# A transfer in four parts, and GpSimd work fenced against VectorE's operations, in a kernel of long convolution and linear attention

## The chip, the cores and the metric

The kernel runs on one core of one Trainium2 chip. TensorE (PE, with its weight loads as PEld), VectorE (DVE), ScalarE (ACT), GpSimd (POOL) and SyncE (SP) run their own queues of instructions in order and wait for each other by semaphores; SP issues every transfer of this kernel. The metric is the device time of one launch in microseconds. Three runs of the kernel before gave 248.29, 248.36 and 249.4; the median is 248.36.

## The reference

Two independent halves work on sequences of S = 2048 positions and D = 576 channels, and are set side by side in the output. All inputs are bfloat16.

```
A:  k_shift = sum over t<4 of k delayed by t, times shift_k[:, t]
    kv = k_shift * v
    y  = causal convolution of kv with ssm_k along S (by FFT of length 2S) + kv * ssm_D
    out[:, :576] = q * y
B:  q, k, v = x @ wqkv, 32 heads of 18
    phi(t) = (t+1 if t>0 else exp(t)) + 1e-6
    num = phi(q) (phi(k)^T v),  den = phi(q) . sum(phi(k)) + 1e-6
    out[:, 576:] = (num / den) @ wo
```

## The kernel before

**Half A.** Channels are cut into five pieces (`HP`): four of 128 and one of 64. For each piece and each half of the positions, `conv_piece` makes four tap products at once (L413, "tap"), adds them in two steps (L418 "tap+", L421, called "tapx" here), and multiplies by v (L424, "tapv"). The convolution is a transform in two stages. `s1` multiplies by the table Gsb on PE (L501) and copies out of PSUM ("s1ev"); `s2` transposes blocks on DVE (L518) and does a small transform on PE (L527). For the filter the same happens ("h": L451, then s1), with a transposing transfer ("trq", L476) and L484 in place of the block transpose for the pieces of `HDMA`. The spectra are then worked on in nine slices of 64 channels, g = 0 to 8: `inv` has two transfers exchange the filter spectrum's rows within SBUF ("X"), makes two products of 128 x 2048 (L548, "p0" and "p1", on DVE or POOL), and transforms back on PE (L558, "i1"), copied into U[vg] ("i1ev").

Slices 0 to 3 fill U0, slices 4 to 7 fill U1, each 128 x 8192 elements (2 MB). In U the partition is 32 kh + something, and the next stage needs another index on the partitions. So `inv2` turns the corner by way of DRAM: one transfer writes U[vg] to `v_scr` (L595, "Vw"), four read it back in another order into V[vg] (L599, "Vr"). Then i2 on PE with table Esb (L611) and the product with q on DVE (L621, "i2q"), and two stores ("yo"). Slice 8 has its own short way without DRAM.

**Half B.** `kproj` and `qproj` (L644, L662) are matmuls of five; phi is an Exp on ACT (L647, L670) and one DVE operation with min and max (L650 "kphi", L673 "qphi"). `b_G` makes G = x^T phi(k) in ten groups of sixteen matmuls (L700, evacuated at L712 or L714). From it come kv, z, den and its reciprocal (L799), M, and broadcasts of the reciprocal ("bc", L827). EPS is added to phi(q): for four of nine tiles by POOL ("pqe", L845), which then multiplies by the copied broadcast ("pqg", L837), for the others within one DVE operation (L841). `b_out` makes sixteen row blocks of the output, two groups of five matmuls each (L861, "out"), copied to `ob` on ACT or DVE ("oev") and stored ("oo").

**What sets the order.** Every piece of work is an entry of a program with a number. The strings PLAN, PLACES and FILL at the end of the file give the order of all entries with the engine of each (P, A, D, G for POOL, S for SP), the place of every buffer, and how many filler matmuls on a zero tile `fz` (L909) stand ahead of an entry. They were made by a planner from the costs written beside each entry, such as `_dve(n)` or `TPOOL`; nothing of it is decided at run time. So an engine that waits holds up all that is behind it in its queue. Two entries by line:

```
595:  load("Vw", None, lambda e: dma(ap(V_d[vg], 0, [[32 * n, 4], [128 * n, 32], [1, 32 * n]]),
596:                                 U[vg].t[:].rearrange("p k c -> p (k c)")), 8192 * n, rd=[U[vg]],
845:  P.op(("POOL", TPE), lambda e, c=c, gp=gp: nc.gpsimd.tensor_scalar_add(out=pq(c, gp), in0=pq(c, gp), scalar1=EPS),
```

Of the kernel before, what the change touches and what calls it, by code (L numbers as in the profile page):

```python
# [15 lines left out]
EPS = 1e-6  # L16
# [189 lines left out]
def _dve(n, rate=1):  # L206
    return 0.145 + n * 0.001045 / rate


def _dma(nb, row=4096):  # L210
    return nb / (16.0 * row / (8.0 + row * 0.0412) * 1000.0)
# [3 lines left out]
def kernel(  # L215
# [45 lines left out]

    def psb(banks, name):
        return P.buf(name, [128, banks, 512], FP32, space="ps", banks=banks)
# [3 lines left out]
    neg1 = SB("neg1", [128, 1], FP32, side=1, pre=True)  # L267
    Gsb = SB("Gsb", [128, 16, 2, 128], side=1, pre=True)
# [133 lines left out]
    def conv_piece(pc, bh):  # L402
# [4 lines left out]
        def tap(e):  # L407
            base = kb.t[:, 8 * bh:8 * bh + 8, c0:c0 + n]
            i0 = bass.AP(tensor=base.tensor, offset=base.offset,
                         ap=[list(base.ap[0]), [D, 4], [D, 8], [1, n]])  # L410
            w = Wj.t[:, 3:4, c0:c0 + n]
            i1 = bass.AP(tensor=w.tensor, offset=w.offset, ap=[list(w.ap[0]), [-D, 4], [0, 8], [1, n]])
            nc.vector.tensor_tensor(out=m.t[:], in0=i0, in1=i1, op=ALU.mult)  # L413
# [3 lines left out]
        P.op(("DVE", _dve(16 * n, 2)),  # L417
             lambda e: nc.vector.tensor_tensor(out=m.t[:, 0:2], in0=m.t[:, 0:2], in1=m.t[:, 2:4], op=ALU.add),  # L418
             wr=[m], name="tap+", bias=bias)
        P.op(("DVE", _dve(8 * n, 2)),  # L420
             lambda e: nc.vector.tensor_tensor(out=m.t[:, 0], in0=m.t[:, 0], in1=m.t[:, 1], op=ALU.add),  # L421
             wr=[m], name="tap+", bias=bias)
        P.op(("DVE", _dve(8 * n, 2)),
             lambda e: nc.vector.tensor_tensor(out=vt.t[:, 8 * bh:8 * bh + 8, c0:c0 + n], in0=m.t[:, 0],  # L424
# [116 lines left out]
    def inv(g, su, bias):  # L541
# [5 lines left out]
        for x, wr in ((1, [(tx, ("x", 0)), (tx, ("x", 1))]), (0, [(tx, 0), (tx, 1)])):  # L547
            P.op({"DVE": _dve(2048, 2), "POOL": TPOOL}, lambda e, x=x: (nc.vector if e == "DVE" else nc.gpsimd).tensor_tensor(  # L548
# [38 lines left out]
    def inv2(vg, bias):  # L587
# [5 lines left out]
        if vg in DR:  # L593
            dtok = P.buf("vd%d" % vg, [128, 1], space="dram")
            load("Vw", None, lambda e: dma(ap(V_d[vg], 0, [[32 * n, 4], [128 * n, 32], [1, 32 * n]]),  # L595
                                           U[vg].t[:].rearrange("p k c -> p (k c)")), 8192 * n, rd=[U[vg]],
                 wr=[dtok], bias=bias, row=8192)
# [246 lines left out]
    for c, gp in PQG:  # L844
        P.op(("POOL", TPE), lambda e, c=c, gp=gp: nc.gpsimd.tensor_scalar_add(out=pq(c, gp), in0=pq(c, gp), scalar1=EPS),  # L845
             wr=[(pqT, (c, 2 * gp + i)) for i in range(2)], name="pqe", bias=("bc", 0.0))
# [42 lines left out]
    P.op(("POOL", 0.35), lambda e: nc.gpsimd.memset(fz.t[:], 0.0), wr=[fz], name="fz", bias=1200)  # L889
# [7 lines left out]
    with tc.manual_schedule():  # L897
        cnt = 0
        for o in order:
# [10 lines left out]
            o.fn(o.eng)  # L910


T16 = 0.28
TPOOL = 4.9
TPQ = 2.6
TPE = 1.3
# [4 lines left out]
9:10 416:3 105:9 99:2 33:9 150:3 444:1 474:1 471:1 451:1 549:1 294:2 309:1 501:2 518:1 568:1 602:2 336:2 598:1 651:1  # L921
703:1 692:7
# [3 lines left out]
G5 S6 G8 G13 S7 S406 S52 G1 S53 G95 G2 S54 G3 S32 G717 S18 G4 S15 P9 S14 P11 S31 A10 A12 P407 G277 S16 P409 D408 A410  # L926
S17 D411 P416 S19 P412 S45 A417 P414 P418 D415 A413 S44 P25 P23 P26 P22 A419 S42 D27 P28 G0 S20 D24 A29 D420 G30 S47
P105 D424 P111 A106 P114 D107 A112 P96 D113 A115 P102 D116 A97 S428 D55 P117 A103 P421 A118 P108 A423 D104 A422 P99
D56 S43 A109 A100 D98 D57 D110 P33 S534 D58 P34 S46 P36 A35 P39 D101 P526 D59 P37 A40 P522 A38 P120 A527 D119 P129 D60
S478 A121 G41 P425 A130 D122 A427 D61 P150 S429 D75 A426 P141 P132 A151 S545 G48 A142 P135 S546 A133 P156 D143 A523  # L930
D134 D76 P138 A136 A157 S49 P147 D137 A139 D77 P144 A148 D140 P123 A145 D78 D146 P126 D131 A124 G271 D62 S535 P162 S50
A127 D125 D79 P240 A163 S273 P180 A241 P430 D149 A181 D128 P432 A431 D182 P174 D80 A433 P183 S272 P186 D434 A175 D158
P171 A184 D81 A187 P177 D185 A172 D176 P168 S275 A178 G51 D173 D188 P195 A169 D179 D164 P204 S453 A196 D170 D152 P210
A205 D82 P524 A211 D206 P207 A525 D87 P213 A208 P198 A214 P528 D215 A199 D212 P192 A529 D209 D200 P216 D88 A193 P189
S454 A217 P165 D194 A190 D218 S710 D89 P225 A166 S479 D197 P222 A226 D90 P159 A223 D227 S503 D224 P455 D167 A160 P457
D191 A456 P219 D161 P201 D530 A458 A220 P480 D459 D242 A202 P482 D221 A481 P228 D203 S21 D483 P531 A229 D484 D541 P237
A533 D230 P231 S662 A532 D91 P153 A238 G537 S274 P243 A232 D92 A154 D239 P542 D155 A244 P259 D233 A544 D245 D93 A543
D71 P251 D94 G547 D72 D73 P246 D74 D252 A253 D83 P266 D247 D248 D84 G536 P256 D267 A268 D85 D86 P234 D63 A257 A260
A258 P504 A235 P261 A505 D236 G548 D64 P506 A262 A263 P254 D508 D65 A507 D66 D67 P509 A255 P515 P513 P511 A514 P264
A512 D516 S276 D68 P460 A265 P466 A461 D510 P464 D69 P249 A467 D70 S517 A465 P437 D250 P439 D438 P441 A440 P435 D442  # L940
P462 A436 P491 D463 A492 P554 S443 P487 A555 P552 D488 P556 A553 P489 D557 P485 A490 P558 S468 D486 P269 A559 D571
P646 A270 P538 D560 S473 A647 P584 A539 P586 D540 A587 P444 D585 P446 A445 P582 S493 D447 A583 P588 P278 A589 D590
P561 S448 P282 A562 D601 P642 A643 P474 D280 D281 A563 D283 P644 D279 P648 D645 A475 P471 S564 P476 D649 S565 S498
D472 P469 A477 P284 A470 D650 P572 D285 G300 S606 D286 A573 S594 P451 D574 P449 G303 A452 P496 D450 P494 A497 G567
D287 P549 S576 A495 S575 P292 A551 S686 P296 S625 A293 S624 P294 A297 P288 A295 P290 A289 P298 D550 G578 A291 P309
S605 A299 P322 D577 P499 A310 S595 P312 D323 A500 P306 D313 A307 P501 P316 A502 P324 D566 P304 G308 A317 P520 S635
D325 S636 A521 P518 D305 P314 A519 P614 G302 D315 P319 A615 S654 P616 S655 D320 G301 P612 A617 P618 D613 A619 P579
G311 A581 D580 P568 A569 D570 P602 A604 P336 D620 S663 P333 A603 P326 D337 D334 G608 P338 D607 A327 P331 P621 D339
A332 P341 D631 S340 A622 S335 P328 D342 A623 P632 D329 P343 D634 S330 A633 P358 A344 P356 D626 G637 A359 S345 P591
A357 P348 D638 A593 S360 P351 S667 A592 S666 D349 P609 D352 S664 D627 P361 A610 P363 D611 A362 P628 A364 G318 P353  # L950
S365 D596 A630 S665 P346 A629 P681 D597 P683 A347 P639 A354 D684 S350 P679 S355 D682 A640 P677 D680 G321 A641 P598
D678 P668 S685 A599 D600 P670 P651 D671 S687 P386 D669 A652 P672 D653 P674 P371 D673 G656 P403 A372 D657 P383 P381
A384 D404 D387 P391 A382 D675 P401 S385 A392 S676 P398 D402 P376 D399 P396 A377 P660 A397 S400 P658 A661 S689 S691
# [49 lines left out]
```

## Time and profile before

| what | before |
|---|---|
| median of three runs | 248.36 us |
| profiled execution, its own time | 247.67 us |
| its span | 245.8 us |
| PE busy, share of the span | 168.9 us, 69% |
| DVE busy | 175.2 us, 71% |
| ACT busy | 124.2 us, 51% |
| POOL busy | 71.4 us, 29% |
| moved by DMA | 40.51 MB, mean 165 GB/s |
| mean granted TensorE clock | 0.886 |

The busy shares are means over stages with different limits. A line of the chain that ended last reads: start, length, what. In a group's line stand source line, engine, operation, what it writes and reads, shapes and count, then busy time and mean length in ns of one, and the idle time before it. The DMA share is the mean busy share of sixteen DMA engines; it can pass 1 where packets overlap.

### The profile page before, as it was taken

What the parts mean: (1) busy time and instruction counts of PE and PEld (TensorE: products, weight loads), DVE (VectorE), ACT (ScalarE), POOL (GpSimd) and SP (SyncE); (2) the same over time, 40 slices, a digit from 0 to 9 for tenths busy, and PEclk for the clock granted to TensorE, in tenths of its full rate; (3) what the DMA queues carried; (4) which work ended last, traced back from release to release, by engine and by line L of the source; (5) the groups of instructions that cost most, each with busy time, mean ns of one, the idle gap of its engine ahead of it and who ended that gap; (6) DMA issues with size and microseconds to landing.
All of it is one profiled execution on the core that took longest, in us unless ns stands there. A gap on an engine that the chain in (4) does not pass through costs nothing.

```text
span 245.8 us, 4335 instructions
## 1 busy us (share of the span) xinstructions
PE 168.9 (69%) x1777; PEld 113.6 (46%) x1787; DVE 175.2 (71%) x192; ACT 124.2 (51%) x173; POOL 71.4 (29%) x37
## 2 busy tenths in 40 slices
PE   2979798999939169999977866774302968700390
PEld 1666563766517046888733433542101546600270
DVE  0179998999999988979899999799600794000352
ACT  2558796787950004488989999472400621300110
POOL 9010000000099900000019999759200060000000
PEclk9999999999997858999999999997955897965568
DMA  5999998993390000199997932243227834222895
GB/s 162 321 333 362 328 296 208 218 214 90 96 265 0 0 3 0 21 225 150 203 200 232 286 149 98 53 112 109 83 83 229 266 97 120 75 91 101 241 288 186
DMA packets 51144, 40.51 MB, mean 165 GB/s; under 512 B 25204, under 2 KB 47989, under 8 KB 50229
## 3 DMA queue, kind: packets, MB, share of 16 engines
q1 hardware_dynamic: 51124, 40.24, 61.3%
q8 instruction: 14, 0.23, 0.4%
q14 instruction: 6, 0.04, 0.1%
HBM read 21.62 MB, written 8.91 MB: 124 GB/s over the span
## 4 chain that ended last, share of the span: by engine, by line
DMA 39%; PE 23%; DVE 22%; issue 6%; ACT 6%; SPq 1%; DVEq 0%; ACTq 0%
DMA v_scr<-U 26%; PE ps_all L700 7%; DVE m L413 5%; DMA kb<-in_A_k_dram 5%; PE ps_all L501 4%; DMA V<-v_scr 3%; PE ps_all L611 3%; DMA Gsb<-tab_g 3%; DVE pk L650 3%; DVE pqT L673 3%; DVE v L424 3%; DMA xT<-in_B_x_dram 2%; DVE m L418 2%; PE ps_all L644 2%; PE ps_all L662 2%
## 5 line engine op out<-in xcount | busy, mean ns | idle before, releaser
L548 POOL TENSOR_TENSOR TT<-su,TT 128x2048 bf16<-128x2048 bf16 x9 | 40.6, 4524 | 47.7 <-issue 24.3
L611 PE MATMUL ps_all<-V,Esb 128*128 128x256 bf16 x64 | 11.3, 338 | 32.7 <-DMA V<-v_scr 32.7
L700 PE MATMUL ps_all<-pk,x_sb 128*128 128x288 bf16 (+1 forms) x160 | 25.5, 326 | 11.1 <-ACT GT L712 7.2
L861 PE MATMUL ps_all<-M,pqT 128*128 128x288 bf16 x128 | 23.9, 319 | 8.5 <-DVE ob L257 6.8
L255 ACT ACTIVATE ob<-ps_all 128x288 bf16<-128x288 f32 x20 | 7.9, 412 | 40.9 <-PE ps_all L861 21.5
L621 DVE TENSOR_TENSOR q<-ps_all,q 128x512 bf16<-128x512 f32 x18 | 11.7, 685 | 21.8 <-PE ps_all L611 21.8
L700 PEld LDWEIGHTS <-x_sb 128*128 128x128 bf16 x160 | 17.4, 110 | 18.0 <-issue 11.5
L548 DVE TENSOR_TENSOR TT<-su,TT 128x2048 bf16<-128x2048 bf16 x9 | 25.0, 2790 | 0.0
L413 DVE TENSOR_TENSOR m<-kb,Wj 128x4096 bf16<-128x4096 bf16 (+1 forms) x10 | 24.6, 2457 | 0.3 <-DMA kb<-in_A_k_dram 0.2
L611 PEld LDWEIGHTS <-Esb 128*128 128x128 bf16 x64 | 7.3, 118 | 36.5 <-issue 19.1
L845 POOL TENSOR_SCALAR pqT<-pqT 128x1024 bf16<-128x1024 bf16 x4 | 11.1, 2770 | 43.1 <-DVE TT L257 42.8
L644 PE MATMUL ps_all<-wk,xT 128*128 128x288 bf16 x160 | 22.0, 286 | 0.8 <-DMA wk<-in_B_wqkv_dram 0.8
L257 DVE CAST ob<-ps_all 128x288 bf16<-128x288 f32 x12 | 5.1, 446 | 24.4 <-DMA out_dram<-ob 21.4
L861 PEld LDWEIGHTS <-pqT 128*128 128x128 bf16 x128 | 13.2, 107 | 15.3 <-issue 9.1
L501 PEld LDWEIGHTS <-Gsb 128*128 128x128 bf16 x320 | 17.9, 99 | 3.8 <-issue 2.7
L255 ACT ACTIVATE U<-ps_all 128x1024 bf16<-128x1024 f32 x10 | 10.1, 1027 | 17.7 <-PE ps_all L558 17.6
L662 PE MATMUL ps_all<-xT,wq 128*128 128x512 bf16 x74 | 18.6, 379 | 0.4
L255 ACT ACTIVATE TT<-ps_all 128x1024 bf16<-128x1024 f32 x15 | 18.0, 1261 | 0.9 <-PE ps_all L484 0.9
L644 PEld LDWEIGHTS <-xT 128*128 128x128 bf16 x160 | 15.3, 98 | 6.4 <-issue 1.5
L909 PE MATMUL ps_all<-fz 128*128 128x256 bf16 x62 | 11.8, 303 | 8.7 <-POOL fz L889 4.4
L647 ACT ACTIVATE ek<-ps_all,neg 128x288 bf16<-128x288 f32 x32 | 15.4, 507 | 3.3 <-PE ps_all L644 2.5
L255 ACT ACTIVATE su<-ps_all 128x1024 bf16<-128x1024 f32 x15 | 14.8, 1022 | 3.1 <-PE ps_all L527 3.0
(99 smaller groups left out, 324.8 us busy)
## 6 DMA issues: line engine op xcount, KB each, us to landing
TT<-TT SPq DMA_DIRECT2D x18, 256.0 KB, 3.0
v_scr<-U SPq DMA_DIRECT2D x2, 2048.0 KB
V<-v_scr SPq DMA_DIRECT2D x8, 512.0 KB, 5.1
x_sb<-in_B_x_dram SPq DMA_DIRECT2D x4, 576.0 KB, 10.4
kb<-in_A_k_dram SPq DMA_DIRECT2D x2, 1152.0 KB, 11.1
v<-in_A_v_dram SPq DMA_DIRECT2D x2, 1152.0 KB, 11.3
out_dram<-ob SPq DMA_DIRECT2D x16, 144.0 KB, 6.1
q<-in_A_q_dram SPq DMA_DIRECT2D x2, 1024.0 KB, 7.0
```

The lines of the kernel that those rows point to most:

```text
L255: nc.scalar.activation(out=o, in_=i, func=ACTF.Copy)
L413: nc.vector.tensor_tensor(out=m.t[:], in0=i0, in1=i1, op=ALU.mult)
L501: nc.tensor.matmul(pf[:, n * j:n * j + n], lhsT=Gsb.t[:, 8 * bg + j, ri, :], rhs=src(8 * bg + j), start=True, stop=True)
L548: P.op({"DVE": _dve(2048, 2), "POOL": TPOOL}, lambda e, x=x: (nc.vector if e == "DVE" else nc.gpsimd).tensor_tensor(out=tx.t[:, x], in0=su ...
L611: nc.tensor.matmul(ps.t[:, 0, n * j:n * j + n], lhsT=Esb.t[:, b, ri, :], rhs=v_, start=(ri == 0), stop=(ri == 1))
L621: nc.vector.tensor_tensor(out=qs, in0=ps.t[:, 0, :].rearrange("p (j c) -> p j c", c=n), in1=qs, op=ALU.mult)
L644: nc.tensor.matmul(ps.t[:, 0, 0:HALF], lhsT=xT.t[:, t, 128 * (r % 4):128 * (r % 4) + 128], rhs=wk.t[:, t, HALF * hh:HALF * hh + HALF], sta ...
L647: P.op(("ACT", _act(HALF) + 0.085), lambda e, hh=hh, ps=ps: nc.scalar.activation(out=eb.t[:, hh], in_=ps.t[:, 0, 0:HALF], func=ACTF.Exp, b ...
L662: nc.tensor.matmul(ps.t[:, 0, :], lhsT=wq.t[:, t, 128 * c:128 * c + 128], rhs=xTg[g].t[:, t, :], start=(t == 0), stop=(t == 4))
L700: nc.tensor.matmul(ps.t[:, 0, 0:n], lhsT=x_sb.t[:, r, FT[t]:FT[t] + 128], rhs=pk.t[:, r, HALF * hh:HALF * hh + n], start=(r == 0), stop=(r ...
L861: nc.tensor.matmul(ps.t[:, 0, 0:HALF], lhsT=pqT.t[:, c, 128 * r:128 * r + 128] if c < 4 else pqt.t[:, 128 * (r % 8):128 * (r % 8) + 128], ...
L909: nc.tensor.matmul(b.t[:, 0, 0:256], lhsT=fz.t[:, 0:128], rhs=fz.t[:], start=True, stop=True)
```

## The change

- The write of U to `v_scr` is four transfers, one for each 32 partitions, in place of one. The bytes and their addresses in DRAM are the same.
- Tap sums and the product with v may go to POOL as well as DVE; in the new PLAN 4 "tap+", 4 "tapx" and 6 "tapv" are POOL's. The addition of EPS may go to ACT; three of four do.
- The costs by which the planner reckons POOL are new (`_pool`), as are T16, TPQ, TPE.
- When a POOL entry of the list `PORT` follows a DVE entry of that list in the order, it waits for that DVE instruction to end. DVE entries get no such wait.
- `fz` is set by DVE, and a constant `epsf` of EPS is set by POOL.
- PLAN, PLACES and FILL are new as a whole: all queues have another order, and many copies out of PSUM another engine.

```diff
+def _pool(n):
+    return 0.07 + n * 0.00196
...
+    def tt(e):
+        return (nc.vector if e == "DVE" else nc.gpsimd).tensor_tensor
+
+    def add_eps(e, o):
+        if e == "ACT":
+            nc.scalar.activation(out=o, in_=o, func=ACTF.Identity, bias=epsf.t[:])
+            return None
+        return nc.gpsimd.tensor_scalar_add(out=o, in0=o, scalar1=EPS)
...
-        P.op(("DVE", _dve(16 * n, 2)),
-             lambda e: nc.vector.tensor_tensor(out=m.t[:, 0:2], in0=m.t[:, 0:2], in1=m.t[:, 2:4], op=ALU.add),
+        P.op({"DVE": _dve(16 * n, 2), "POOL": _pool(16 * n)},
+             lambda e: tt(e)(out=m.t[:, 0:2], in0=m.t[:, 0:2], in1=m.t[:, 2:4], op=ALU.add),
              wr=[m], name="tap+", bias=bias)
-        P.op(("DVE", _dve(8 * n, 2)),
+        P.op({"DVE": _dve(8 * n, 2), "POOL": _pool(8 * n)},
...
-            P.op({"DVE": _dve(2048, 2), "POOL": TPOOL}, lambda e, x=x: (nc.vector if e == "DVE" else nc.gpsimd).tensor_tensor(
+            P.op({"DVE": _dve(2048, 2), "POOL": _pool(2048)}, lambda e, x=x: tt(e)(
                 out=tx.t[:, x], in0=su.t[:], in1=tx.t[:, x], op=ALU.mult), rd=[su], wr=wr, name="p%d" % x, bias=bias)
...
-            load("Vw", None, lambda e: dma(ap(V_d[vg], 0, [[32 * n, 4], [128 * n, 32], [1, 32 * n]]),
-                                           U[vg].t[:].rearrange("p k c -> p (k c)")), 8192 * n, rd=[U[vg]],
-                 wr=[dtok], bias=bias, row=8192)
+            for kh in range(4):
+                load("Vw", None, lambda e, kh=kh: dma(
+                    ap(V_d[vg], 32 * n * kh, [[128 * n, 32], [1, 32 * n]]),
+                    U[vg].t[32 * kh:32 * kh + 32].rearrange("p k c -> p (k c)")), 2048 * n, rd=[U[vg]],
+                    wr=[(dtok, kh)], bias=bias, row=8192)
...
-        P.op(("POOL", TPE), lambda e, c=c, gp=gp: nc.gpsimd.tensor_scalar_add(out=pq(c, gp), in0=pq(c, gp), scalar1=EPS),
-             wr=[(pqT, (c, 2 * gp + i)) for i in range(2)], name="pqe", bias=("bc", 0.0))
+        P.op({"ACT": _act(1024), "POOL": TPE}, lambda e, c=c, gp=gp: add_eps(e, pq(c, gp)),
+             rd=[epsf], wr=[(pqT, (c, 2 * gp + i)) for i in range(2)], name="pqe", bias=("bc", 0.0))
...
-            o.fn(o.eng)
+            got = o.fn(o.eng)
+            if o.name in PORT and o.eng in ("DVE", "POOL"):
+                if o.eng == "POOL" and port is not None:
+                    tc.add_manual_dep(got.ins, port.name, mybir.DependencyInfo(
+                        mybir.DependencyClass.Sync, mybir.DependencyReason.DATA), reason="port")
+                port = got.ins if o.eng == "DVE" else None
...
+PORT = ("tap", "tap+", "tapx", "tapv", "p0", "p1", "pqg", "pqe")
```

## The prediction

> **What bounds the kernel now.** I read the chain that ended last first. One line of it outweighs all others, and the same chain in order of time gives the two places.
>
> ```profile
> DMA v_scr<-U 26%; PE ps_all L700 7%; DVE m L413 5%; DMA kb<-in_A_k_dram 5%; PE ps_all L501 4%; DMA V<-v_scr 3%; PE ps_all L611 3%; DMA Gsb<-tab_g 3%; DVE pk L650 3%; DVE pqT L673 3%; DVE v L424 3%; DMA xT<-in_B_x_dram 2%; DVE m L418 2%; PE ps_all L644 2%; PE ps_all L662 2%
> ...
> 152.17 32.55 DMA v_scr<-U
> 184.77 4.24 DMA V<-v_scr
> ...
> 195.64 31.93 DMA v_scr<-U
> 227.66 3.92 DMA V<-v_scr
> ```
>
> A write of 2 MB takes 32.55 us; reading the same bytes back starts to land after 4.24. Why, the stretches say (columns: stretch, length, busy time of PE, PEld, DVE, ACT, POOL with counts, granted clock, DMA share, GB/s):
>
> ```profile
> 153.00:159.00 6.00, 4.81 (x50) 3.38 (x51) 4.28 (x4) 2.78 (x5) 5.09 (x2) 1.00 0.25 55
> 210.00:222.00 12.00, 3.84 (x49) 3.30 (x47) 0.00 (x0) 0.99 (x2) 0.00 (x0) 0.79 0.25 86
> 232.00:236.00 4.00, 4.00 (x19) 2.61 (x18) 1.38 (x2) 0.50 (x2) 0.00 (x0) 0.50 1.14 347
> ```
>
> While only the write runs, the DMA share is 0.25: four of sixteen engines, at 55 GB/s (14 each) early and 86 (22 each) late. In the read the share is over 1 and 347 GB/s move. In 210 to 222 DVE does nothing at all: nothing covers the second write.
>
> Next the timeline of DVE and POOL between 66 and 87, where the engine sums say DVE is full:
>
> ```profile
> 67.96 4.44 DVE L418 TENSOR_TENSOR m<-m 128x1024 bf16<-128x1024 bf16 x1
> ...
> 74.47 2.11 DVE L421 TENSOR_TENSOR m<-m 128x512 bf16<-128x512 bf16 x1
> 76.51 5.08 DVE L413 TENSOR_TENSOR m<-kb,Wj 128x2048 bf16<-128x2048 bf16 x1
> 81.51 4.26 DVE L424 TENSOR_TENSOR v<-m,v 128x512 bf16<-128x512 bf16 x1
> 85.70 0.68 DVE L418 TENSOR_TENSOR m<-m 128x1024 bf16<-128x1024 bf16 x1
> ...
> 67.03 18.46 POOL L548 TENSOR_TENSOR TT<-su,TT 128x2048 bf16<-128x2048 bf16 x4 [18.67 <-ACT su L255]
> ```
>
> The same L418 takes 4.44 beside POOL and 0.68 once POOL is done at 85.5: a DVE operation with two SBUF inputs stands still until POOL's current one ends. The four cost 3.76 + 1.68 + 3.9 + 3.84 = 13.2 us. The nine products on DVE lose too (2.79 mean, 1.21 at best, so 14 us in all), in this group's row:
>
> ```profile
> L548 DVE TENSOR_TENSOR TT<-su,TT 128x2048 bf16<-128x2048 bf16 x9 | 25.0, 2790 | 0.0
> ```
>
> Last the stretch up to the first write. ACT is busy 43.7 of 48.8 us and DVE 45.7, DVE's share swollen by the port; ACT's queue waits for nothing but 2.5 us of it.
>
> ```profile
> 103.34:152.17 48.83, 41.29 (x591) 26.85 (x593) 45.68 (x44) 43.74 (x48) 23.45 (x8) 1.00 0.87 195
> ```
>
> **The change part by part.** The sum is made against the profiled execution: span 245.8, its own time 247.67; the median of the runs shown is 248.36, so 0.7 is added at the end.
>
> *First write.* Four transfers of 32 rows of 16 KB replace one whose DRAM side had an outer count of 4. If an outer count of 32 reaches all engines, 2.1 MB moves at 16 x 22 = 352 GB/s (6.0 us) or at 16 x 14 = 220 (9.5 us), by the rows of 86 and 55 GB/s. I take the slow one: there, as in every new transfer, engines work inside the same 32 or 64 partitions. Adding 0.6 for an issue and about 1.5 between last byte and release (4.24 for the first read's 0.5 MB, which moves in 1.5 at 347, leaves 2.7 for both), a write takes 8.5 to 12; I take 11.5. The 4-KB-row transfers point the same way: 256 KB into 64 adjacent partitions land in 7.0 (hs), into 64 alternating ones in 3.0 (TT).
>
> [...]
>
> Four more entries in SP's queue cost 3 x 0.6; behind them stand only output stores (oo) and the reads, which need all four. From U0 complete to the first read landed: 11.5 + 4.2 = 15.7, not 36.8. New cover in that gap, counted in the new queues: ACT 15.2, PE 13.8, DVE 12.8 us, so with 11.5 the write is just hidden, and a faster one gives little: ACT is late next. Gain 21.1.
>
> *Between the writes.* Before, U1 was complete 6.6 us after the first read landed, behind four i2 groups. Now i1 of piece 7 is behind two: two groups 0.9, i1 0.7, two q products and the U copy on DVE (0.6 + 0.6 + 1.1): 3.3. Gain 3.3.
>
> *Second write.* Same 11.5, plus 0.5 as its fourth part stands on SP behind a yo store that waits for a q product. 31.93 + 3.92 become 12 + 4.2. PE has 16.8 us queued behind piece 7 (17 out groups of 0.61, 5 i2, piece 8), so again about covered. Gain 19.6.
>
> *Tail.* First read landed to last q product took 9.5 us with ten out matmuls left over and a granted clock of 0.50 to 0.63; eight i2 groups (3.6) paced by four reads 1.6 apart give 6.5. The last store and end stay 4.7. Gain 3.
>
> *Up to the first write.* Counted in the two orders, 4 tap+, 4 tapx and 6 tapv leave DVE: at 1.13, 0.60 and 0.60 from start to start, half that where a piece is 64 wide, 9.5 us. On POOL they cost 4.06 (L548's fastest 2048) or 2.1 (the fastest 1024, L837). Each is fenced behind the listed DVE operation before it in the order. Nothing fences DVE: its next listed operation still waits for POOL. In the new order 2 to 5 us of unlisted DVE work (kphi 0.37, qphi 0.60, copies) stands between in most places; I count losses of 0.3, 0.5, 1.7 (two POOL sums before tapv of conv3) and 1.1 (conv8). So 13.2 of stalls become 3.6. The bounds are 0, if POOL always ends within that work, and 13.2 again, if it starts late each time; the count is the nearer. Behind a fenced POOL sum stand POOL's next sums, then tapv, which s1 of u reads tens of us later, and the 0.51 memsets of x's tail (L340), for which k groups of the next 512 rows wait; they stand 10 to 40 PE entries further on.
>
> DVE is then no longer late; PE is. Until 66.7 us PE and DVE ran even (PE 51.4 us of work, so 15.3 behind the start). The new PE queue up to its ninth G group holds 76 us by the rows: 32 k groups (0.61), 16 q (1.09), 2 q tails (1.2), 9 G (2.03), 10 h transposes (0.62), 12 s1 (0.45), 10 x transposes (0.28), the rest 5. 76 + 15.3 = 91.4. The loads add: wo (0.58 MB) and x group 3 now go ahead of k's second half, xT2's tail and hs; at the page's 321 to 362 GB/s these 1.2 MB are 3.3 us, of which PE, at xT2's first reader near 41, has 1 in hand if xT2 lands as late as the 39 to 40 of before. With 2.5: 94, against 103.3 before for the same place. Gain 9.3.
>
> From there to U0 complete ACT's queue is the bound: 46.4 us of work took 48.8; now 48.4, since three EPS additions (1.03 each, from the copies of 1024) came to ACT and a few copies shifted. POOL has 42.2 us there, in 51: not the bound, though close. What the products on DVE stop losing lies beside ACT's work here and beside the writes later, so it counts nothing. Loss 2. U0 complete at 94 + 51 = 145 (152.2 before). The one fz memset on DVE and PE's 25 more filler matmuls (0.11 each) stand in waits: nothing, at most 1.
>
> *Sum.* 21.1 + 3.3 + 19.6 + 3 + 9.3 - 2 = 54.3; 247.67 - 54.3 = 193.4, plus 0.7: 194.
>
> **The rivals.** (1) *Full-rate writes.* 8.5 each instead of 11.5; ACT's 15.2 and PE's 16.8 us of cover eat most: 2 + 2 us, and if xT2 also lands in time 2.5 more: 187. (2) *Something new waits before U0.* The trq transposes and the wv load on SP now stand between exchanges; kv waits for wv (6.7 us to land, issued only after h4's transpose at about 101), and every 2048-long POOL product now fenced behind a DVE one delays an i1 that PE meets in order. Each slip is 2 to 6 us; two or three of them: 205 to 212. For it: POOL at 42 of 51 us. Against it: i1 of pieces 0 to 3 is last in the stretch. (3) *The writes aren't spread.* If a write still takes 32: 194 + 2 x 20.5 = 235. The share of 0.25 with an outer count of 4 speaks against it. (4) *Slower than before.* One mechanism: fewer engines per transfer than four, since a quarter of the partitions is served by a quarter of the engines and the four parts run one after another. Two engines at 22 GB/s need 48 us and 50 with the ends; 194 + 2 x 38.5 = 271. It decides from a write of 38.5 us on (194 + 2 x 27 = 248), 55 GB/s, the early rate of four engines. Against it: the 64-partition hs loads land in 7.0 for 256 KB, far faster than 44 GB/s would allow if all were in one quarter.
>
> **How the numbers follow.** Forecast 0.60, own range 189 to 201; (1) 0.13; (2) 0.20; (3) 0.03; (4) 0.04. The range 184 to 212 leaves out (3), (4) and the ends of (1) and (2), under 2 in 10. About 0.5% is what a measurement of this kernel can tell from no change (runs of before lie 0.4% apart). Faster: all but (4) and a shade of (3): 0.95; same 0.01; slower 0.04.
>
> **What would show it.** A DMA share near 1 and 200 to 360 GB/s while v_scr is written, each write 8 to 12 us from issue to landing; no L418 or L424 above 3 us; the first v_scr write issued at 145 (140 to 150); ACT busy over nine tenths from 94 on; U1 complete 18 to 20 us after U0. Wrong if a write takes over 15, if PE stands in the k projections for loads for more than 5 us, or if POOL's products release i1 late.

## The result and the profile after

The changed kernel takes 200.22 us (median of four runs, 196.29 to 200.92) against 248.36: ratio 0.794, 95% interval 0.786 to 0.802. The ratio is taken from the two undisturbed executions, 196.29 and a further one of 198.33 (granted clock 0.957 and 0.954, mean 197.3 us); the other three, at 0.944 to 0.946, took 200.02 to 200.92. The same file on another chip gave 198.13 (196.97 to 200.31). The profiled execution is the 196.29 one; its span is 194.5.

Lines of the changed kernel have other numbers: L413, L418, L421 and L424 are L427, L432, L435 and L438 there, L548 is L562, L611 is L627; the runs below shift some of them by a few lines. L247 and L251 are the helper that issues transfers. "The port" is short for what the rows of before show: a DVE operation with two inputs in SBUF stands while a POOL operation runs (L418 on 128x1024 took 4.44 us beside POOL and 0.68 without).

The head of the page of the changed kernel:

```profile
span 194.5 us, 4394 instructions
...
PE 163.6 (84%) x1803; PEld 113.9 (59%) x1812; DVE 152.1 (78%) x182; ACT 123.1 (63%) x174; POOL 86.1 (44%) x47
...
DVE 28%; DMA 27%; PE 19%; ACT 11%; SPq 7%; issue 5%; DVEq 0%; ACTq 0%
DMA wq<-in_B_wqkv_dram 8%; DMA V<-v_scr 7%; DVE m L427 6%; SPq L251 6%; DMA wk<-in_B_wqkv_dram 4%; ACT TT L259 4%; DMA v<-in_A_v_dram 4%; DMA v_scr<-U 4%; PE ps_all L877 4%; PE ps_all L660 3%; DVE hT L477 3%; PE ps_all L678 3%; DVE ct L532 2%; DVE U L261 2%; DVE pqT L689 2%
```

The writes were 26% of the chain; what is left of them is 4%. POOL went from 71.4 to 86.1 us of work and DVE from 175.2 to 152.1: it gave sums away and stands less beside POOL (its products take 1.21 us each, not 2.79).

SP's timeline shows the first corner turn (start, length, what, count), and the chain in order of time both:

```profile
143.38 4.75 SPq L251 DMA_DIRECT2D v_scr<-U  x4
148.22 4.99 SPq L251 DMA_DIRECT2D out_dram<-ob  x4
154.00 4.50 SPq L251 DMA_DIRECT2D V<-v_scr  x4
```

```profile
146.16 7.76 DMA v_scr<-U
...
156.40 8.07 DMA V<-v_scr
164.51 1.03 PE ps_all L627 x8
...
176.82 5.17 DMA V<-v_scr
182.04 1.86 PE ps_all L627 x8
```

U0 is complete at 143.4, not 152.2. From the first issue of the write to the first read that may start is 10.6 us (143.38 to 154.00), not 32.6. The stretches of the changed kernel (columns: stretch, length, busy time of PE, PEld, DVE, ACT, POOL with counts, granted clock, DMA share, GB/s): the way from the ninth G group to U0, the first write, the second.

```profile
95.78:143.38 47.60, 40.14 (x622) 25.04 (x624) 44.17 (x44) 46.14 (x54) 41.47 (x14) 1.00 0.65 168
...
143.38:153.90 10.52, 10.46 (x164) 7.01 (x160) 10.52 (x11) 10.23 (x18) 0.48 (x1) 1.00 0.88 242
161.90:176.70 14.80, 14.22 (x146) 11.35 (x144) 8.99 (x13) 6.04 (x12) 4.07 (x1) 1.00 1.01 267
```

In the writes of before the DMA share was 0.25 and in the second of them DVE idled; now the share is 0.88 and 1.01 and PE is busy 10.46 of 10.52 and 14.22 of 14.80 us. In the second write, 14.80 us at 267 GB/s are 3.95 MB, of which 2.1 are U1: the rest is stores and the last 0.24 MB of the first reads.

### The profile page after: what moved, and what is told of

It is laid out like the page before. It is cut to its first block, busy times and chain, and to the rows that moved or that the text cites. A ratio compares the mean times of both kernels' runs of the same rounds, so it can differ in the third digit from the quotient of the medians.

```text
span 194.5 us, 4394 instructions
## 1 busy us (share of the span) xinstructions
PE 163.6 (84%) x1803; PEld 113.9 (59%) x1812; DVE 152.1 (78%) x182; ACT 123.1 (63%) x174; POOL 86.1 (44%) x47
## 4 chain that ended last, share of the span: by engine, by line
DVE 28%; DMA 27%; PE 19%; ACT 11%; SPq 7%; issue 5%; DVEq 0%; ACTq 0%
DMA wq<-in_B_wqkv_dram 8%; DMA V<-v_scr 7%; DVE m L427 6%; SPq L251 6%; DMA wk<-in_B_wqkv_dram 4%; ACT TT L259 4%; DMA v<-in_A_v_dram 4%; DMA v_scr<-U 4%; PE ps_all L877 4%; PE ps_all L660 3%; DVE hT L477 3%; PE ps_all L678 3%; DVE ct L532 2%; DVE U L261 2%; DVE pqT L689 2%
## 5 line engine op out<-in xcount | busy, mean ns | idle before, releaser
L562 POOL TENSOR_TENSOR TT<-su,TT 128x2048 bf16<-128x2048 bf16 x8 | 32.4, 4070 | 12.4 <-ACT su L259 9.4
L432 POOL TENSOR_TENSOR m<-m 128x2048 bf16<-128x2048 bf16 (+1 forms) x4 | 14.3, 3577 | 22.0 <-DVE m L427 14.9
L427 DVE TENSOR_TENSOR m<-kb,Wj 128x4096 bf16<-128x4096 bf16 (+1 forms) x10 | 20.6, 2071 | 0.0
L663 ACT ACTIVATE ek<-ps_all,neg 128x288 bf16<-128x288 f32 x32 | 15.8, 500 | 7.6 <-PE ps_all L660 6.6
L716 PE MATMUL ps_all<-pk,x_sb 128*128 128x289 bf16 (+1 forms) x160 | 20.6, 287 | 0.0
L877 PE MATMUL ps_all<-M,pqT 128*128 128x288 bf16 x128 | 20.0, 286 | 0.0
L637 DVE TENSOR_TENSOR q<-ps_all,q 128x512 bf16<-128x512 f32 x18 | 11.8, 686 | 10.1 <-PE ps_all L627 7.5
L716 PEld LDWEIGHTS <-x_sb 128*128 128x128 bf16 x160 | 15.3, 98 | 4.2 <-issue 0.2
L686 ACT ACTIVATE eq<-ps_all,neg 128x512 bf16<-128x512 f32 x18 | 12.4, 689 | 7.7 <-PE ps_all L678 6.9
L666 DVE SCALAR_TENSOR_TENSOR pk<-ek,ps_all 128x288 bf16<-128x288 bf16 x32 | 13.4, 445 | 3.3 <-ACT ek L663 3.3
L259 ACT ACTIVATE Cu<-ps_all 128x1024 bf16<-128x1024 f32 (+1 forms) x16 | 15.3, 1026 | 0.0
L435 POOL TENSOR_TENSOR m<-m 128x1024 bf16<-128x1024 bf16 x4 | 8.5, 2128 | 15.0 <-DVE m L432 15.0
L627 PE MATMUL ps_all<-V,Esb 128*128 128x256 bf16 x64 | 9.6, 299 | 6.4 <-DMA V<-v_scr 6.4
L438 POOL TENSOR_TENSOR v<-m,v 128x1024 bf16<-128x1024 bf16 (+1 forms) x6 | 11.9, 1977 | 6.4 <-DVE m L427 6.2
## 6 DMA issues: line engine op xcount, KB each, us to landing
v<-in_A_v_dram SPq DMA_DIRECT2D x2, 1152.0 KB, 13.3
```

The costliest lines, as they stand in the source:

```text
L259: nc.scalar.activation(out=o, in_=i, func=ACTF.Copy)
L427: return nc.vector.tensor_tensor(out=m.t[:], in0=i0, in1=i1, op=ALU.mult)
L432: lambda e: tt(e)(out=m.t[:, 0:2], in0=m.t[:, 0:2], in1=m.t[:, 2:4], op=ALU.add),
L562: P.op({"DVE": _dve(2048, 2), "POOL": _pool(2048)}, lambda e, x=x: tt(e)(out=tx.t[:, x], in0=su.t[:], in1=tx.t[:, x], op=ALU.mult), rd=[su ...
L663: P.op(("ACT", _act(HALF) + 0.085), lambda e, hh=hh, ps=ps: nc.scalar.activation(out=eb.t[:, hh], in_=ps.t[:, 0, 0:HALF], func=ACTF.Exp, b ...
L666: P.op(("DVE", _dve(HALF)), lambda e, hh=hh, ps=ps: nc.vector.scalar_tensor_tensor(out=pk.t[:, r, HALF * hh:HALF * hh + HALF], in0=eb.t[:, ...
```

## The experiments

Three theories stood at the start. The four-part write gains by using sixteen engines (against: the new order and the fence made most of it). Parts of 32 adjacent partitions run at half rate (against: a write is as fast as it gets). Up to U0 ACT is the bound (against: DVE at the port, or late loads).

### The four-part write alone

The kernel before, with its one entry issuing four transfers; no queue is changed.

```diff
-            load("Vw", None, lambda e: dma(ap(V_d[vg], 0, [[32 * n, 4], [128 * n, 32], [1, 32 * n]]),
-                                           U[vg].t[:].rearrange("p k c -> p (k c)")), 8192 * n, rd=[U[vg]],
+            def vw(e):
+                for kh in range(4):
+                    dma(ap(V_d[vg], 32 * n * kh, [[128 * n, 32], [1, 32 * n]]),
+                        U[vg].t[32 * kh:32 * kh + 32].rearrange("p k c -> p (k c)"))
+            load("Vw", None, vw, 8192 * n, rd=[U[vg]],
```

> The kernel before, with only the corner-turn write cut into four transfers of 32 rows; all queues in the old order. Theory (the two writes are the bulk of the gain): each write falls from 32 to 10 to 12 us, as the 10.5 us measured in the changed kernel; the old order has less work queued behind the first write, so of 2 x 21 us nearly all appears: 204 to 212 us. Rival (the new order is what pays, the writes were only long because nothing was queued): no more than 20 us gained, 228 or more.

212.46 us (210.5 to 213.66), ratio 0.854 [0.850, 0.858]. SP's timeline and the stretches of the two writes:

```profile
152.87 4.96 SPq L247 DMA_DIRECT2D v_scr<-U  x4
165.97 2.44 SPq L247 DMA_DIRECT2D V<-v_scr  x3
```

```profile
153.00:164.00 11.00, 9.11 (x98) 5.83 (x97) 8.65 (x10) 5.89 (x10) 6.37 (x3) 0.84 0.92 199
181.00:193.00 12.00, 8.96 (x61) 6.48 (x60) 9.45 (x10) 3.07 (x6) 4.05 (x1) 0.86 0.99 227
```

The split alone is worth 36 us of the change's 48 (51 by the mean of 197.3). Each write takes 13.1 to 13.3 us (10 to 12 were expected), 2.5 more than the first write of the changed kernel has. The outer count on the DRAM side is 32 here and was 4 before; the DMA share is 0.92 and 0.99 here and was 0.25 before.

### The change with a single write

The new order, fence and engines; the first of the four entries writes all, as before, and the others write nothing.

```diff
-                    ap(V_d[vg], 32 * n * kh, [[128 * n, 32], [1, 32 * n]]),
-                    U[vg].t[32 * kh:32 * kh + 32].rearrange("p k c -> p (k c)")), 2048 * n, rd=[U[vg]],
+                    if kh == (0, 2)[vg]:
+                        dma(ap(V_d[vg], 0, [[32 * n, 4], [128 * n, 32], [1, 32 * n]]),
+                            U[vg].t[:].rearrange("p k c -> p (k c)"))
```

> The changed kernel, with the write put back into one transfer whose DRAM side has an outer count of 4, at the place of the first of the four. Theory: each write takes 30 to 33 us again, share 0.25 while it is alone; 200 + 2 x 19 = 236 to 244 us. Rival (the new order would cover a long write): below 225.

240.19 us (239.52 to 242.23), ratio 0.967. The chain and two stretches inside the writes:

```profile
143.53 32.30 DMA v_scr<-U
175.88 4.38 DMA V<-v_scr
```

```profile
153.00:172.00 19.00, 3.09 (x51) 1.78 (x49) 3.26 (x5) 3.87 (x7) 4.20 (x2) 0.63 0.27 87
195.00:215.00 20.00, 4.22 (x51) 3.47 (x48) 0.00 (x0) 0.38 (x1) 0.00 (x0) 0.68 0.26 87
```

U0 is complete at 143.5, as in the change: the 9 us ahead of the first write belong to order, engines and fence, and 8 us is what they are worth by themselves. The two parts add up to 36 + 8 = 44; the other 4 (7 by the mean of 197.3) come only together. Work moved beside the writes may be the reason; no run sets it apart.

### No fence

```diff
-                if o.eng == "POOL" and port is not None:
-                    tc.add_manual_dep(got.ins, port.name, mybir.DependencyInfo(
-                        mybir.DependencyClass.Sync, mybir.DependencyReason.DATA), reason="port")
```

> The changed kernel without the waits of GpSimd on VectorE's listed operations; order and data dependencies as they are. Theory (the order alone keeps the two apart, and the fence is a small help): GpSimd starts some sums and products under a VectorE operation, VectorE's listed operations lose 2 to 6 us in all, most of it beside PE and ACT: 0 to 3 us slower than with the fence (196 to 203). Rival (the fence is what keeps the port free): VectorE loses over 10 us and the time rises above 206.

206.67 us (205.06 to 208.52), ratio 0.829 [0.824, 0.834]; the first write is issued at 150.3 instead of 143.4. Groups of DVE by shape, of the changed kernel and then of the run without the fence (count, busy us, mean ns):

```profile
L562 DVE TENSOR_TENSOR TT<-su,TT 128x2048 bf16<-128x2048 bf16 x10 | 11.8, 1206 | 0.0
L432 DVE TENSOR_TENSOR m<-m 128x2048 bf16<-128x2048 bf16 x5 | 6.7, 1347 | 0.0
```

```profile
L562 DVE TENSOR_TENSOR TT<-su,TT 128x2048 bf16<-128x2048 bf16 x10 | 16.1, 1634 | 0.0
L432 DVE TENSOR_TENSOR m<-m 128x2048 bf16<-128x2048 bf16 x5 | 11.4, 2272 | 0.0
```

```profile
94.94 5.00 DVE L432 TENSOR_TENSOR m<-m 128x2048 bf16<-128x2048 bf16 x1
```

The same work costs DVE 9 us more in these two groups, with one operation of 5.00 us where the form takes 1.2 to 1.9 in the changed kernel. By the two ratios the kernel loses about 9 us (6.5 between the medians). The result lies at the edge between the two expectations and nearer to the rival: the fence is no trifle. Of the 8.8 us by which the change completes U0 earlier, the new order and engines without the fence have 1.9 (150.3 for 152.2).

### One flat write of 128 rows

DRAM rows follow the partitions, so one transfer with an outer count of 128 on both sides writes U.

```diff
+                    if kh == (0, 2)[vg]:
+                        dma(ap(V_d[vg], 0, [[32 * n, 128], [1, 32 * n]]),
+                            U[vg].t[:].rearrange("p k c -> p (k c)"))
```

> The changed kernel with one write of all 128 rows, laid out one after another in DRAM, so that sixteen engines serve all partitions at once; rows then stand in another order than the corner turn needs, the reads are as before and the values of half A are others. Theory (32 adjacent partitions halve the rate): the write takes 6.5 to 8 us from issue to landing where the four parts took 10.5, at 300 GB/s or more, and packets of 16 KB take 0.6 us. Rival (writing DRAM is the limit): 10 us as in four parts.

The reads are left as they are and fetch other rows of the same number, so half A's values end in other places in this run; the bytes moved and the work done are the same. 189.79 us (189.11 and 190.47), ratio 0.763 [0.757, 0.769]. SP's timeline and a stretch inside the first write:

```profile
141.22 0.35 SPq L251 DMA_DIRECT2D v_scr<-U  x1
149.82 3.96 SPq L251 DMA_DIRECT2D V<-v_scr  x4
```

```profile
143.00:147.00 4.00, 4.00 (x47) 2.89 (x45) 4.00 (x6) 4.00 (x8) 0.00 (x0) 1.00 0.95 391
```

391 GB/s, against 199 in the first stretch of the four-part run above. The packets show where that comes from (16-KB packets of v_scr's write in groups of 32 in order of start; median time of one in us, and the time from the first packet's start to the last one's end):

```
run, write                     parts in order    median by group        first to last
split alone, first             0, 1, 2, 3        1.27 1.27 1.12 1.27    11.7
split alone, second            0, 1, 2, 3        1.27 1.29 1.07 1.27    11.2
changed kernel, first          0, 3, 1, 2        1.27 0.96 0.63 0.97     9.3
corner turn first (below), 2nd 2, 3, 1, 0        1.10 1.27 1.08 1.24    11.1
flat, first                    all rows          0.61 0.63 0.61 0.63     6.6
```

With the share near 1 (0.92 in the first write of the split alone) and the engines inside one part of 32 rows a packet takes twice as long as in the flat write: 16 x 16.4 KB in 1.27 us is 206 GB/s, in 0.61 it is 430. By the table a part that follows one of the other half of the partitions (0 then 3, 3 then 1, 1 then 2) has a median of 0.63 to 1.12 us, one that follows a part of its own half (0 then 1, 2 then 3, 1 then 0) 1.24 to 1.29. That the tail of one part and the head of the next overlap there at the better rate is the author's reading; the order alone was not varied in a run of its own.

The write is 2.0 us shorter (8.6 instead of 10.6, with 6.5 to 8 expected) and the second one's packets run in 6.9 instead of 12.5. What hangs on the write comes earlier with it: U1 is complete 16.2 us after the write's issue, not 18.5. The second write, issue to first read, takes 11.8 instead of 14.9. From the first issue of a write to the end of the span are 46.1 us here, 51.1 in the profiled change and 53.1 in its repeat. The writes are 2.0 + 3.1 us of that; the granted clock of the stretch, 0.99 here and 0.94 and 0.92 there, may be part of the rest. U0 was complete at 141.2, 2 us earlier, ahead of any difference in the writes; why is open.

### The reads by 32 partitions

To let the flat write keep every value in its place, four reads each bring all 32 rows into 32 adjacent partitions.

```diff
-                load("Vr", V[vg], lambda e, bq=bq: dma(V[vg].t[:, 8 * bq:8 * bq + 8, :], ap(
-                    V_d[vg], 8 * bq * 128 * n, [[n, 128], [128 * n, 8], [1, n]])), 2048 * n, rd=[dtok],
+                load("Vr", V[vg], lambda e, bq=bq: dma(V[vg].t[32 * bq:32 * bq + 32, :, :], ap(
+                    V_d[vg], 1024 * n * bq, [[n, 32], [32 * n, 32], [1, n]])), 2048 * n, rd=[dtok],
```

> The corner turn with one flat write of 128 rows, as in the run with the flat write, and reads that do the rest: four reads of 32 partitions, each with all 32 rows, in place of four reads of 128 partitions with 8 rows each, so that every value ends in its place. The write should take 8.5 to 9 and the second 11.5 to 12.5 us. Theory that the writes alone made the gain of the flat run: 190 to 193 us. Rival, that the reads now pay what the writes saved, since each goes into 32 partitions and an i2 group needs all four instead of one: first read landed to first q product grows from 5.5 to 9 or more, kernel 197 to 202.

211.86 us (211.56 to 212.91), ratio 0.854: worse than either. Stretches inside the reads, of the changed kernel and then of this run:

```profile
157.00:161.00 4.00, 1.63 (x40) 0.99 (x41) 1.57 (x3) 0.52 (x1) 1.50 (x1) 1.00 1.10 297
```

```profile
157.00:165.00 8.00, 0.60 (x5) 0.25 (x3) 1.22 (x1) 1.40 (x3) 3.16 (x2) 0.72 1.19 181
```

The share is about the same, the rate 181 instead of 297 GB/s: a 512-byte packet takes 51 ns instead of 27 to 31. PE's first i2 matmul waits until 167.5, 13.8 us behind the first read's issue; in the change it is 4.7 (154.00 to 158.71). Two things add up in this: the packets are slower, and the first i2 group now needs all four reads. In the change the last of the four lets its i2 groups start at 164.5, 10.5 us behind the first issue, so the slower packets alone are about 3.3 us of a turn. What the write gained, the reads lost several times over. The rival's mechanism held and its size fell short (197 to 202 expected).

### All 128 rows on both ways

The last run keeps the flat write and reads row 32 kh + k into partition 4 k + kh, so each read goes into every fourth partition; the table of the second stage has its rows in that order, and slice 8's evacuations write in it too. With it go the edits of hD, corner turn and loads below.

```diff
+                def vr(e, bq=bq):
+                    h, r0 = 2 * (bq % 2), 16 * (bq // 2)
+                    for kh in (h, h + 1):
+                        dma(V[vg].t[kh:128:4, r0:r0 + 16, :],
+                            ap(V_d[vg], 1024 * n * kh + 32 * n * r0, [[n, 32], [32 * n, 16], [1, n]]))
...
+                    e, sp.t[:, 0, 4 * hh:4 * hh + 4, :, t].rearrange("p w (k h) -> p w h k", h=4),
```

> All 128 rows on both ways, with every value in its place. The write is one flat transfer of 128 rows, as in the flat run. The reads put row 32 kh + k of the old order into partition 4 k + kh, so each goes into every fourth partition instead of 32 adjacent ones, and the constant table of the second inverse stage has its rows in the same order; eight reads of 0.25 MB, in two halves of 16 rows. Also in it, from the earlier runs: hD ahead of the GpSimd sums, the corner turn ahead of the stores in SP's queue, wo and x group 3 later. Theory that 32 adjacent partitions were what made the reads slow in the run with reads by 32 partitions (182 to 215 GB/s, 13 us for 2 MB): the reads take 8 to 10 us again, the write 8.6, and the kernel 187 to 193 us. Rival, that runs of 32 partitions are slow wherever they lie, because of their DRAM side (32 rows 16 KB apart) or their size: reads of 12 us or more and 203 to 211 us.

201.75 us (200.33 to 202.86), ratio 0.814 [0.811, 0.818]; the expected 187 to 193 did not come. A stretch inside the reads, and ACT's group of the new evacuations:

```profile
162.00:168.00 6.00, 2.53 (x61) 1.46 (x73) 1.99 (x3) 2.18 (x4) 3.95 (x2) 0.99 1.00 281
```

```profile
L259 ACT ACTIVATE TT<-ps_all 128x512 bf16<-128x512 f32 x4 | 9.5, 2648 | 0.0
```

On the packets the theory held, on the length of the reads not quite: from the first issue to the last landing they take 11.1 us (159.44 to 170.53), where 8 to 10 were expected and the rival had 12 or more. 32 partitions spread over the 128 take 512 bytes in 27 ns, at 281 GB/s, with the same DRAM rows 16 KB apart: adjacency was the cause, not the number of partitions nor the DRAM side. From the first write's issue to the end are 47.8 us, 3.3 to 5.3 less than in the change. But the four copies for slice 8, which write 2 bytes in every 16, take 2.65 us each where two of 1.31 to 1.38 stood. That is 7 to 8 us more of ACT, which PE waits for (3.9 us at one place, 2.3 at another), and the write is issued at 150.8 instead of 143.4. The granted clock from 100 to there is 0.90 instead of 1.00, so the 7.4 us are not all shown to be ACT's. A layout that saves the corner turn's time was found, and not a way to feed it cheaply.

### hD ahead of the GpSimd sums

The one-partition operation L477 reads two SBUF inputs and is not in the list PORT. It took 3.84 us beside a POOL sum and 0.37 without. Timelines of DVE and of POOL in the changed kernel:

```profile
51.10 0.68 DVE L689 SCALAR_TENSOR_TENSOR pqT<-eq,ps_all 128x512 bf16<-128x512 bf16 x1
51.70 3.84 DVE L477 TENSOR_TENSOR hT<-hT,Drow 1x128 bf16<-1x128 bf16 x1
55.47 0.44 DVE L666 SCALAR_TENSOR_TENSOR pk<-ek,ps_all 128x288 bf16<-128x288 bf16 x1
```

```profile
51.26 4.05 POOL L432 TENSOR_TENSOR m<-m 128x2048 bf16<-128x2048 bf16 x1 [7.63 <-DVE m L427]
```

```diff
-PORT = ("tap", "tap+", "tapx", "tapv", "p0", "p1", "pqg", "pqe")
+PORT = ("hD", "tap", "tap+", "tapx", "tapv", "p0", "p1", "pqg", "pqe")
...
-... P201 D79 ... G80 P210 A181 D434
+... P201 D434 D79 ... G80 P210 A181
...
-... D88 A456 ... A505 D459
+... D88 A456 D459 ... A505
```

> In the changed kernel hD (L477, a one-partition operation that the fence's list leaves out) stood still for 3.84 us at 51.70 and 1.84 us at 79.61 beside a GpSimd sum. Here it goes ahead of the sum in both places and is on the list. The stalls should be gone by every theory (mean of L477 from 1566 ns to under 1000). Theory that DVE is on the path there: U0 complete and the whole kernel 3 to 5 us earlier. Rival, that PE sets the pace up to 100 (busy 10.00 us in every 10 from 70 on): 0 to 1.5 us.

The stalls are gone (longest L477 now 1.14 us), U0 is complete at 143.3 as before, the kernel takes 197.24 us (195.56 to 198.11) beside 198.13 for the unchanged file on the same chip. Ratios 0.798 [0.785, 0.810] and 0.802 [0.792, 0.812]: not told apart. In place of the first stall DVE now waits, by its timeline:

```profile
52.88 0.67 DVE L689 SCALAR_TENSOR_TENSOR pqT<-eq,ps_all 128x512 bf16<-128x512 bf16 x1
55.59 0.46 DVE L666 SCALAR_TENSOR_TENSOR pk<-ek,ps_all 128x288 bf16<-128x288 bf16 x1 [2.04 <-ACT ek L663]
```

Its next product wants an Exp that ACT has only then. About 5 us of standing cost nothing that these runs can tell.

### The corner turn ahead of the stores

```diff
-... S691 D674 P651 S688 D672 S335 P675 A652 S690 ...
+... S691 D674 P651 S690 S688 D672 S335 P675 A652 ...
...
-... A367 S679 ... P658 S694 D661 S696 S695 ... A377 S697
+... A367 S694 S696 S695 S697 S679 ...
```

> The second write took 14.8 us, the first 10.6, and the fourth part of the second stood on SP behind a yo and an oo store until 169.57, 7.7 us after U1. Here that part is issued with its three sisters and the four reads go ahead of the stores that stood before them. Theory that the place in SP's queue made the difference: write 10.5 to 11.5 us, kernel 3 to 4 us shorter. Rival, that other traffic and the 32-partition transfers themselves made it, or that PE's own out groups fill the gap: write 13 us or more, or kernel within 1 us.

197.77 us (195.28 to 198.39): no change. The second write went from 14.9 to 13.1 us (162.54 to 175.61), not to 10.6. Its stretch:

```profile
162.54:175.61 13.07, 12.62 (x135) 10.19 (x133) 7.17 (x11) 4.72 (x10) 4.07 (x1) 1.00 1.01 252
```

PE has work for 12.62 of the 13.07 us and the engines are full; 252 GB/s are 3.3 MB, 1.2 of them other transfers, mostly stores. The place in SP's queue was 1.8 us of the second write's excess and cost nothing that these runs can tell; the parts' order (2, 3, 1, 0, by the table above) and the stores are left for the rest, and no run sets the two apart.

### Loads later

```diff
-... P22 S274 D424 ... P102 S21 A38 ... D125 S49 P240 ... A169 S20 D527 ...
+... P22 D424 ... P102 A38 ... D125 S49 S21 P240 ... A169 S20 S274 D527 ...
```

> In the changed kernel the loads of wo and of x group 3 stand in SP's queue ahead of what the first stages need: the second half of v landed at 47.9, the third piece of x at 54.15, and PE waited 3.3 us for it. Here both loads are put behind (wo behind the load that followed, x group 3 behind the X transfers). Theory, late loads on the path: PE's wait for x shrinks by 2 us or more and U0 is complete 2 to 3.5 us earlier, kernel the same amount shorter. Rival, ACT's full stretch from 100 to 143 or the port's waits set U0 anyway: less than 1 us.

196.14 us (194.52 to 197.66), ratio 0.788 [0.782, 0.794]: the lowest median of all runs but the flat one, and its interval overlaps the change's own. U0 is complete at 142.3, 1 us earlier. PE's waits up to 70 us, in the changed kernel and then here:

```profile
PE ps_all L660 <- DMA xT<-in_B_x_dram: 3.3, 1, 3.3
...
PE ps_all L465 <- DMA hs<-in_A_ssm_k_dram: 0.4, 1, 0.4
```

```profile
PE ps_all L465 <- DMA hs<-in_A_ssm_k_dram: 3.0, 1, 3.0
...
PE ps_all L660 <- DMA xT<-in_B_x_dram: 1.4, 1, 1.4
```

x's wait shrank by 1.9 us and another, for hs, grew by 2.6. The wait changed its name, and the 1 us at U0 lies nearer to the rival than to the theory.

### ACT more, and ACT less

Up to U0 the rows show ACT full; two runs push at it from both sides. First, each copy of the broadcast on ACT is done twice.

```diff
-            P.op(either(1024), lambda e: copy(e, bb.t[:], ps.t[:]), rd=[ps], wr=[bb], name="bcev", bias=("bc", 0.0))
+            P.op(either(1024), lambda e: [copy(e, bb.t[:], ps.t[:]) for _ in range(2 if e == "ACT" else 1)], rd=[ps], wr=[bb], name="bcev", bias=("bc", 0.0))
```

> Each copy of bcev that runs on ACT is done twice: three more ACT operations of about 1.07 us, 3.2 us of ACT time between 100 and 143. Nothing else is changed. Theory, ACT is the bound there (busy 9.93 to 10.00 us in every 10): U0 complete 2.5 to 3.5 us later, kernel 2.5 to 3.5 us longer. Rival, DVE or GpSimd sets the end of U0 and ACT only looks full: less than 1 us.

201.65 us (200.31 to 203.69) beside 198.13 on the same chip, 3.5 more for 3.2 of work. The first write is issued at 147.4, 4.2 later than in the repeat. Stretches from 100 to U0, of the changed kernel and of this run:

```profile
100.00:143.38 43.38, 35.97 (x566) 22.02 (x568) 39.95 (x39) 42.89 (x48) 38.89 (x13) 1.00 0.62 157
```

```profile
100.00:147.35 47.35, 39.96 (x555) 22.99 (x540) 39.92 (x38) 46.03 (x51) 38.55 (x13) 0.89 0.57 142
```

ACT does 46.03 in place of 42.89, and the granted clock of the stretch is 0.89 instead of 1.00, which gives PE the same work at 39.96 instead of 35.97. ACT's idle time in the stretch is still only 1.3 us (0.5 before), so 3.1 of the 4.2 us are its added work; the rest may be the clock's. Then the other direction: one EPS addition from ACT to POOL, one copy from ACT to DVE.

```diff
-... A301 D279 ... P586 A587 ... G577 ... G566 ...
+... D279 ... P586 D587 ... G577 ... G301 G566 ...
```

> The other direction of the doubled copies: one pqe goes from ACT to GpSimd's idle 2.3 us at 122, and one copy of Cu from ACT to DVE's idle 2.4 us at 120.5. ACT has 2.35 us less to do between 100 and 143. Theory, ACT is the bound there: U0 complete 1.2 to 2.3 us earlier and the kernel 1 to 2.3 us shorter. Rival, DVE (busy 9.6 to 10.0 in every 10 from 130 on) is as full and takes its place: less than 0.7 us.

200.4 us (196.75 to 201.07), four runs that give no verdict: one at a granted clock of 0.958 took 196.75, beside 196.29 and 198.33 for the change, and the three others, the profiled one among them, ran at 0.935 to 0.942. U0 is complete at 146.4 in that profile:

```profile
100.00:146.41 46.41, 38.12 (x571) 23.32 (x568) 41.57 (x40) 41.84 (x46) 42.43 (x14) 0.93 0.60 149
```

```profile
PE ps_all L515 <- POOL v L438: 2.0, 1, 2.0
```

ACT has 4.6 us of waits now, POOL is the fullest engine with 42.43, and PE waits 2.0 for POOL's tapv. So adding to ACT lengthens the stretch; whether relieving it shortens it stays open. In the change ACT at 42.9, DVE at 40.0 and POOL at 38.9 of 43.4 us are nearly level, so little room is left on the others. The clock of this stretch differs as well (0.93 for 1.00), and how much of the 3 us is POOL's and how much the clock's the run does not show.

### The change once more

> The changed kernel once more, unedited, as the measure for the three others of this group. Every theory: 196 to 201 us, U0 complete near 143, first write 10 to 11 us.

198.13 us (196.97 to 200.31); first write 10.5 us, U0 at 143.2. Trace and trace differ by up to 2 us after U0 (51.1 and 53.1 to the end), which bounds what one profile of this kernel can tell.

## Why the prediction was right, and where not

The direction, the place of the gain and its size held: 200.22 against 194 (197.3 by the executions behind the ratio), inside the range and inside the forecast's own range of 189 to 201. By steps, profile against profile:

| step | forecast gain | measured | from |
|---|---|---|---|
| up to the first write | 9.3 - 2 = 7.3 | 8.8 | U0 at 143.4 for 152.2 |
| first write | 21.1 | 21.6 | 15.3 us to the first i2 (158.71) for 36.9 |
| between the writes | 3.3 | 3.4 | 3.2 for 6.6 |
| second write | 19.6 | 15.8 | 20.1 (161.91 to 182.04) for 36.0 |
| tail | 3 | 1.7 | 12.5 to the end for 14.2 |
| sum | 54.3 | 51.3 | 194.5 for 245.8 |

- *First write.* 11.5 forecast, 10.6 measured, between the bounds of 8.5 and 12. The two rates behind them, 220 and 352 GB/s, are both there: 391 in the flat write, 206 by the packets inside one part. That an outer count of 32 would reach all engines was an assumption, and the share of 0.88 and 1.01 bears it out. Taking the slow rate for "engines work inside the same 32 or 64 partitions" was right in cause for the new transfers, as the reads into adjacent and spread partitions show (181 and 281 GB/s); which partitions the old write was in at 55 GB/s no trace shows. That the first write came out below 11.5 looks like luck: its parts stand in the order 0, 3, 1, 2, in which the later ones had packets of 0.63 to 0.97 us where the first had 1.27, and the prediction did not look at the order. In other orders a write took 13.1 us and more.
- *The cover.* "With 11.5 the write is just hidden, and a faster one gives little" is the step that failed. In the change PE still waits 2.8 us for the first turn's reads and 2.5 for the second's, and in the flat run a first write shorter by 2.0 us brought U1 2.3 us earlier, where the rival of full-rate writes allowed 2 of 3. The cover counted for ACT was there (10.33 of the write's 10.62 us busy), but PE, with 13.8 us queued for a gap of 15.3, ran out of work first, and what comes after waits for the corner turn, too.
- *Second write.* The size of this term was wrong by 3.8: 14.9 us, not 12 (just short of the 15 that the prediction named as a sign of being wrong), and 5.2 to the first i2, not 4.2. The fourth part's place behind the stores was forecast at 0.5 and is 1.8; the stores beside it and the order of the parts, 2, 3, 1, 0, were left out. Moving the part forward did not shorten the kernel.
- *Tail.* The four reads were issued over 5.6 us, between stores on SP (176.82 to 182.42), where 1.6 between each makes 4.8, and the first two pairs of i2 groups ran in 1.86 and 1.47 us for the 1.03 of the others, the first at a granted clock of 0.50; 8.0 us from first i2 to last product, not 6.5.
- *Up to the first write.* The stalls at the port were counted as 3.6; they are about 5 in L477, which the count passed over since the list did, and about 2 in listed operations (their time over the fastest of the same form: L432 0.7, L435 0.9, L438 0.5). It made no odds: without L477's 5 us nothing changed. The ninth G group ended at 95.8 (94 forecast) and the way from there took 47.6 (51), with ACT busy 46.1 of it. The two errors offset each other, and the sum held in part by luck. The terms listed for PE add up to 77, not 76, which is 1 of the 1.8 us, and the 51.4 us of PE work up to 66.7 stand in no row (the profile of before has PE busy for 57.3 of them). "103.3 before for the same place" is misread, too. The ninth G group of before ends at 107.7; at 103.34 ACT ends two copies of Ch:

```profile
105.59 2.13 PE L700 MATMUL ps_all<-pk,x_sb 128*128 128x288 bf16 x16
```

```profile
102.25 1.09 ACT L255 ACTIVATE Ch<-ps_all 128x512 bf16<-128x512 f32 x2 [0.20 <-PE ps_all L501]
```

By the end of the ninth G group the way up to it gained 11.9 us (9.3 forecast) and the way behind it lost 3.1 (2 forecast).

- *Behind the decimal.* The 0.7 added from span to median was too small: the profiled execution was the shortest of four, and the median lies 3.9 above it, the mean of 197.3 1.0.

Rivals: full-rate writes gave 189.8 in the flat run (187 forecast), at a price that the reads set, so it was the right size for a kernel that this change is not, with 2 us of it from a U0 that came earlier for a reason that stays open. The unspread write gave 240.2 (235 forecast) when it was put back. "Something new waits before U0" did not happen here; in the one profile with one more POOL operation PE waited 2.0 us for a tapv, at a clock that had fallen as well. Fewer engines is out: the share is 0.88 and 1.01. The argument given against it did not hold, though: 256 KB in 7.0 us, ends included, are 37 GB/s, which is less than 44 and not far more.

## What to carry to other kernels

When a transfer runs at a quarter of the DMA share, look at its outer count first (here 0.25 with 4, 0.92 and 0.99 with 32); when it runs at a full share and half the rate, look at which partitions it touches (199 GB/s in the four-part write, 391 in the flat one), on the reading side too (181 into adjacent partitions, 281 into spread ones). A transfer cut into parts is worth a look at the order of the parts (9.3 us and 11.1 to 11.7 here). Whether an engine is the bound is asked from both sides: more work on ACT lengthened the stretch here, and the run with less of it did not settle the other half. A standing engine costs only what stands behind it: 5 us of DVE at the port cost nothing where DVE's next operation waited for ACT anyway, and without the fence 9 us more of standing came with about 9 us more of time.

## What was not expected of the hardware

- The order of transfers over partition groups seems to count. The same four parts took 11.1 to 11.7 us from first to last packet as 0, 1, 2, 3 or 2, 3, 1, 0, and 9.3 as 0, 3, 1, 2, with other transfers beside them that differ, too.
- A read into 32 adjacent partitions took 51 ns for each 512 bytes, into every fourth partition 27, and into all 128 partitions 27 to 31.
- ACT copies of 512 elements that write 2 bytes in every 16 took 2.65 us, against 0.63 for those writing 4 in every 16 (slice 8's `su`, in the same run) and 1.31 to 1.38 for 1024 elements at 2 in every 4. Five nanoseconds an element can undo what a better layout saves.
- A DVE operation on one partition and 128 elements took 3.84 us beside a POOL sum and 0.37 without: it stands like any other.
- Issuing is not free for SP, and the price varies: in the changed kernel's first write the third and fourth part took 1.87 and 1.97 us to issue where the first took 0.35. Why, no run shows.
